# Order of the two projection memory blocks in a fused layernorm, attention and SwiGLU-gate kernel

## Chip, cores and metric

The kernel runs on one core of one Trainium2 chip. The metric is the device time of one execution in microseconds (us), lower is better; the time before is 1717.34 us, the median of three runs from 1717.03 to 1718.39.

## What is computed

Float32 throughout, 2048 tokens of width 512, 32 heads of width 16, a gate of inner width 1792:

```python
xn = layernorm(x)                                 # 2048 x 512
q, k, v = split_heads(xn @ wqkv)                  # 32 heads, 16 wide
s = merge(softmax(q @ k.T * 16**-0.5) @ v) @ wo
g = silu((silu(xn @ w1) * (xn @ w3)) @ w2)        # 512 -> 1792 -> 512
out = x + s * g
```

## The kernel before

Products of float32 values are made from two parts of each value, high and low (suffix `h` and `l`), and three matmuls.

**The projection** (first some 160 us) is the `with` block whose first line the diff touches (L415). It opens two blocks ("pools") of on-chip memory. `pro` holds the eight `wq` tiles (the parts of wqkv, 6 KB per partition each), nine input rows `xin` of 2 KB, some tiny columns and five normalised rows `xn` of 2 KB, 78,240 bytes per partition in all. `pros` holds what leaves the projection: two rows of values `vrow` (2,176 bytes each) and three `sh` and three `sl` of 2 KB, the parts of a block of q or k rows, 16,640 bytes in all. ScalarE copies a finished product from PSUM to `sh` (L575), VectorE makes `sl` (L576), and SyncE's queue stores both to DRAM (L578); for values ScalarE copies to `vrow` (L509), the queue stores that (L510), and ScalarE copies four heads into the resident tile `vt` (L511). The last work of the projection is the value row of the last sixteenth of the tokens: its matmuls (L504), L509, the store L510, L511. Then SyncE's queue loads the next heads' values (`load_v(1)`, L359) and goes on to the gate's weights (L306).

**The main stage** follows without a barrier. When the `with` block ends both its pools are closed, and three pools are opened in their place, one above the other from the same bottom address: `ring` (the later parts of the gate's weights, ten tiles of 2 KB named `wh4`, `wl4` to `wl8`), `work` (24 tiles `pt` for exponentials, and small ones, 59,648 bytes) and `ffn` (the gate's own tiles `th`, `g`, `hs`, `part`). The framework makes the first instruction that uses a new pool wait for the work on every tile of each closed pool that the new one lies over, not only for the tile under its own address.

PE, the tensor engine, takes half-height matmuls in two lanes: `m` (scores for the row maxima, L388, reduced by VectorE in L390), `e` (transposed scores, L624, to which ScalarE applies the exponential into `pt`, L627), `f` (the gate, L855) and, full, `pv` (L637, the exponentials times the values). Their order is a fixed string, `ORDER_OF_ISSUE`; seven PSUM banks are dealt out in that order, and a matmul that begins a bank waits until the engine that reads the bank's last content is done. So PE runs at most seven results ahead of ScalarE and VectorE. GpSimd (POOL) splits raw gate weights `wr` into parts (L320, L321), in order, with the gate's elementwise work (L724, L725, L740 to L742) between. The first four weight units go to tiles that were there before (`xeh`, `xel`); the fifth, `wh4` and `wl4`, is the first in `ring`.

Of the kernel before, what the change touches and what calls it, by code (L numbers as in the profile page):

```python
# [144 lines left out]
def kernel(ctx: ExitStack, tc: tile.TileContext, x, wqkv, wo, w1, w3, w2, out):  # L145
# [266 lines left out]
            nc.sync.dma_start(raw(qs[p % 2])[r:r + 2, c], raw(turned)[16 * h:16 * h + 16, :])  # L412


    with tc.tile_pool(name="pro", bufs=1) as pro, tc.tile_pool(name="pros", bufs=1) as pros:  # L415
        wsp = [[pro.tile([P, 3 * D], F32R, name=f"wq{v}{k}") for v in "hl"] for k in range(KC)]
        xin = [pro.tile([P, D], F32, tag="xin", name=f"xin{t}", bufs=9) for t in range(4)]

# [919 lines left out]
```

## Time and profile before

| | |
|---|---|
| median of three runs | 1717.34 us |
| the profiled execution's own time | 1718.99 us |
| its span, first to last instruction | 1717.2 us |
| mean granted TensorE clock | 0.999 |
| busy: PE, VectorE (DVE), ScalarE (ACT), GpSimd (POOL) | 100%, 84%, 72%, 45% |
| first matmul of the main stage | 159.83 us |

The time is 1.8 us longer than the span. A row of a timeline gives its start, its length, the engine, the line and operation, how many instructions were merged into it, and in brackets how long the engine had been idle and what it waited for. In a table of windows a row is a stretch, its length, then the busy time of PE, PE's weight loads, DVE, ACT and POOL with their instructions, the granted clock, the busy share of the DMA engines and GB/s. A matmul's modelled length overlaps the next: the distance from start to start counts.

### The profile page before, as it was taken

To read this page: it belongs to the slowest core of one execution; us is meant where nothing else is said; L and a number is where in the kernel's file an instruction comes from. 1 tells how busy PE (TensorE), PEld (TensorE's weight loads), DVE (VectorE), ACT (ScalarE), POOL (GpSimd) and SP (SyncE) were. 2 spreads that over 40 slices of the span, in tenths; PEclk is the share of its full clock that TensorE was granted. 3 is DMA by queue.
4 is the path that set the end of the run, shared out by engine and by line. 5 is a ranking of instruction groups with operands and counts; after the bars stand their busy time and mean duration, and the time that the engine had idled before them with its cause. 6 is when DMAs were issued, how large, how long until landed. Compare 5 with 4: busy or idle time off the path is not lost. (4 is left out here: it accounts for less than half of the span.)

```text
span 1717.2 us, 35614 instructions
## 1 busy us (share of the span) xinstructions
PE 1709.9 (100%) x13204; PEld 1095.6 (64%) x13204; DVE 1445.2 (84%) x2477; ACT 1232.4 (72%) x2408; POOL 764.5 (45%) x793
## 2 busy tenths in 40 slices
PE   9999999999999999999999999999999999999999
PEld 8877666666566656566666666566666666665457
DVE  7566999999899889978897898988898989789836
ACT  4223687777878777788777777787778777777971
POOL 3102655255626660566256533664565426542201
PEclk9999999999999999999999999999999999999999
DMA  8756113132323222232332322123512222241722
GB/s 283 250 205 207 58 45 72 33 82 64 77 77 94 70 63 39 60 71 75 88 93 51 73 54 72 45 75 86 118 51 69 64 55 70 68 106 45 248 67 99
DMA packets 146477, 155.36 MB, mean 90 GB/s; under 512 B 41472, under 2 KB 100864, under 8 KB 143328
## 3 DMA queue, kind: packets, MB, share of 16 engines
q1 hardware_dynamic: 145440, 152.04, 31.8%
q8 instruction: 104, 1.70, 0.4%
q10 hardware_dynamic: 864, 1.05, 0.2%
q14 instruction: 69, 0.57, 0.1%
HBM read 107.97 MB, written 44.02 MB: 89 GB/s over the span
## 5 line engine op out<-in xcount | busy, mean ns | idle before, releaser
L390 DVE TENSOR_REDUCE mp<-m 128x1 f32<-128x512 f32 x2048 | 1286.2, 683 | 171.8 <-PE m L388 87.3
L627 ACT ACTIVATE pt<-e 128x512 f32<-128x512 f32 x2048 | 1073.3, 606 | 275.7 <-PE e L624 161.6
L624 PE MATMUL e<-qs,ks 64*128 64x512 f32 x2048 | 719.8, 410 | 0.2
L388 PE MATMUL m<-ks,qs 62*128 62x512 f32 x2048 | 710.5, 416 | 1.8 <-ACT pt L627 1.6
L637 PE MATMUL pv<-pt,vt 128*17 128x512 f32 x4096 | 491.9, 595 | 0.0
L388 PEld LDWEIGHTS m<-ks,qs 62*128 62x128 f32 x2048 | 335.9, 184 | 158.7 <-ACT pt L627 46.3
L624 PEld LDWEIGHTS e<-qs,ks 64*128 64x128 f32 x2048 | 346.5, 185 | 134.2 <-DVE mp L390 35.1
L637 PEld LDWEIGHTS pv<-pt,vt 128*17 128x17 f32 x4096 | 93.2, 96 | 234.5 <-issue 228.7
L855 PE MATMUL f<-xtl,wh 64*128 64x512 f32 x488 | 176.7, 393 | 0.0
L855 PE MATMUL f<-xth,wl 64*128 64x512 f32 x488 | 175.5, 394 | 0.0
L855 PE MATMUL f<-xth,wh 64*128 64x512 f32 x488 | 174.3, 395 | 0.0
L740 POOL TENSOR_TENSOR h<-g,h 128x512 f32<-128x512 f32 x56 | 71.9, 1285 | 201.5 <-ACT h L736 199.7
L855 PE MATMUL f<-wh,hs 64*128 64x512 f32 x496 | 154.8, 393 | 0.0
L855 PE MATMUL f<-xth,xel 64*128 64x512 f32 x408 | 147.7, 398 | 0.0
L855 PE MATMUL f<-xtl,xeh 64*128 64x512 f32 x408 | 147.3, 393 | 0.0
L855 PE MATMUL f<-xth,xeh 64*128 64x512 f32 x408 | 146.6, 395 | 0.0
L855 PE MATMUL f<-xeh,hs 64*128 64x512 f32 x400 | 124.7, 393 | 0.0
L321 POOL TENSOR_TENSOR wl<-wr,wh 128x512 fp32r<-128x512 f32 x92 | 118.5, 1288 | 7.7
L320 POOL TENSOR_SCALAR wh<-wr 128x512 fp32r<-128x512 f32 x92 | 56.9, 618 | 117.6 <-PE f L855 91.6
L321 POOL TENSOR_TENSOR xel<-wr,xeh 128x512 fp32r<-128x512 f32 x76 | 97.9, 1288 | 6.3
L724 POOL TENSOR_SCALAR th<-th 128x512 f32<-128x512 f32 x56 | 34.6, 618 | 127.9 <-ACT th L717 127.8
L855 PE MATMUL f<-wl,hs 64*128 64x512 f32 x248 | 91.4, 392 | 0.0
(175 smaller groups left out, 2065.3 us busy)
## 6 DMA issues: line engine op xcount, KB each, us to landing
wr<-in_B_w_dram SPq DMA_DIRECT2D x168, 256.0 KB
qs<-qk SPq DMA_DIRECT2D x186, 64.0 KB
ks<-qk SPq DMA_DIRECT2D x90, 128.0 KB
qk<-sh SPq DMA_DIRECT2D x32, 256.0 KB
qk<-sl SPq DMA_DIRECT2D x32, 256.0 KB
v<-vrow SPq DMA_DIRECT2D x16, 272.0 KB
xin<-in_A_x_dram SPq DMA_DIRECT2D x16, 256.0 KB
g<-part SPq DMA_DIRECT2D x16, 256.0 KB
```

The costliest lines, as they stand in the source:

```text
L320: nc.gpsimd.tensor_scalar(hi, t, 1.0, 1.0, op0=ALU.mult, op1=ALU.mult)
L321: nc.gpsimd.tensor_sub(lo, t, raw(hi))
L388: nc.tensor.matmul(ps, qs[p % 2][64 * h:64 * h + KM, q0:q0 + P], ks[p % 2][64 * h:64 * h + KM, c * 512:(c + 1) * 512], start=True, stop=True)
L390: nc.vector.reduce_max(mp[p, half][:, h, qt, c:c + 1], ps, axis=AX.X)
L624: nc.tensor.matmul(ps, ks[p % 2][64 * h:64 * h + KR, k * P:(k + 1) * P], qs[p % 2][64 * h:64 * h + KR, q0:q0 + 512], start=True, stop=True)
L627: nc.scalar.activation(pt, ps, AF.Exp, scale=DH ** -0.5)
L637: nc.tensor.matmul(pv[32 * j:32 * j + VW, :], vt[2 * p // GH][:, key, 2 * p % GH + j % 2, :], pt, start=key < 2 if last else k == 0, stop= ...
L724: nc.gpsimd.tensor_scalar(th, th, 1.0, 1.0, op0=ALU.add, op1=ALU.mult)
L740: nc.gpsimd.tensor_mul(h2, g, h2)
L855: nc.tensor.matmul(ps, left[r], right[r], start=starts and lane == 0, stop=ends and lane == 1)
```

## The change

The two pools are opened in the other order; the tiles, the computation and the instructions are the same.

```diff
-    with tc.tile_pool(name="pro", bufs=1) as pro, tc.tile_pool(name="pros", bufs=1) as pros:
+    with tc.tile_pool(name="pros", bufs=1) as pros, tc.tile_pool(name="pro", bufs=1) as pro:
```

What is opened first lies lowest. By the sizes above, counted in bytes per partition from the bottom of the two:

| | before | after |
|---|---|---|
| `pro` | 0 to 78,240 | 16,640 to 94,880 |
| `pros` | 78,240 to 94,880 | 0 to 16,640 |
| `ring` (0 to 20,480) lies over | `pro` | all of `pros`, 3,840 bytes of `pro` |
| `work` (20,480 to 80,128) lies over | `pro`, 1,888 bytes of `pros` | `pro` |
| `ffn` (from 80,128) lies over | `pros` | `pro` |

Every engine's instructions stand in the order they had; what differs is what the first user of each new pool waits for. Of two engines the places are shown, before with a minus and after with a plus. First ScalarE, where the projection ends and the exponentials begin; `DMAHW0` to `DMAHW7` count finished DMAs, the other names in brackets count finished instructions of an engine:

```order
 L509 COPY vrow_250<-m 128x32x16 [waits PE_49]
 L511 COPY vt<-m 128x4x16
-L627 ACTIVATE pt<-e 128x512 [waits DMAHW3_49,DMAHW2_49,DMAHW4_49,DMAHW1_49,DMAHW5_49,DVE_49,DMAHW6_49,PE_49,DMAHW7_49,Activation_49,Pool_49]
+L627 ACTIVATE pt<-e 128x512 [waits PE_49,Pool_49]
 L627 ACTIVATE pt<-e 128x512 [waits PE_49] x15
 L717 ACTIVATE th<-f 128x512 [waits PE_49]
```

The seven DMA counters stood for the last stores of the `sh`, `sl` and `vrow` tiles (L578 and L510), the last value row's among them. The first exponential no longer waits for any of them, only for PE and for GpSimd's last work on the columns of `pro`.

Then GpSimd, at the fifth weight unit:

```order
 L320 TENSOR_SCALAR xeh<-wr 128x512 [waits DMAHW1_49]
 L321 TENSOR_TENSOR xel<-wr,xeh 128x512 [waits Pool_49]
-L320 TENSOR_SCALAR wh_1723<-wr 128x512 [waits DMAHW3_49,DMAHW4_49,DMAHW2_49,DMAHW7_49,DVE_49,PE_49]
+L320 TENSOR_SCALAR wh_1723<-wr 128x512 [waits DMAHW3_49,DMAHW4_49,DMAHW2_49,DMAHW5_49,DMAHW1_49,DMAHW6_49,DMAHW0_49,DMAHW7_49,DVE_49,Activation_49]
 L321 TENSOR_TENSOR wl_1724<-wr,wh_1723 128x512 [waits Pool_49]
 L320 TENSOR_SCALAR wh_1737<-wr 128x512 [waits DMAHW0_49]
```

The split of the fifth unit (`wh_1723` is `wh4`) now waits for those stores; the load of its raw weights (`DMAHW7`) it waited for before and waits for now. Two waits on the same stores go with it: those of GpSimd's first `th` (L724), and of PE's first `pv` (L637). PE's first use of `wl4` (L855) and VectorE's first `rec` (L651) wait for more or fewer of the same stores.

## Prediction

> **What bounds the kernel.** I read the page first, then the waits of PE over the whole span.
>
> ```profile
> span 1717.2 us, 35614 instructions
> PE 1709.9 (100%) x13204; PEld 1095.6 (64%) x13204; DVE 1445.2 (84%) x2477; ACT 1232.4 (72%) x2408; POOL 764.5 (45%) x793
> ...
> PE m L388 <- ACT pt L627: 1.6, 1, 1.6
> PE pv L447 <- POOL minus L442: 1.4, 1, 1.4
> PE m L504 <- ACT wqh L487: 0.2, 1, 0.2
> ```
>
> PE is busy from end to end, and only three of its waits show as idle time. Two belong to the start of the program. The third, 1.6 us behind an exponential, is the only hole that PE has after the first 10 us. Who caused it is asked of line 627 (its releasers), then of ScalarE's timeline and of the DMA queue's.
>
> ```profile
>   DMA v<-vrow: 2.2, 1
> ...
> 160.42 0.22 ACT L511 COPY vt<-m 128x64 f32<-128x64 f32 x1
> 162.88 3.54 ACT L627 ACTIVATE pt<-e 128x512 f32<-128x512 f32 x7 [2.24 <-DMA v<-vrow]
> 167.50 5.12 ACT L627 ACTIVATE pt<-e 128x512 f32<-128x512 f32 x9 [1.08 <-PE f L855]
> ...
> 160.55 0.32 SPq L510 DMA_DIRECT2D v<-vrow  x1
> 162.63 0.37 SPq L359 DMA_DIRECT2D vt<-v  x1
> 163.10 9.28 SPq L306 DMA_DIRECT2D wr<-in_B_w_dram  x6
> ```
>
> Of 2048 exponentials one waited for a store: the first. ScalarE was done with the projection at 160.42 + 0.22 = 160.64 and stood idle 2.24 us until the last value row, issued at 160.55, had landed. This is the wait that the change takes from ScalarE. What it did to PE stands in PE's timeline (one of the two lanes' rows at each start):
>
> ```profile
> 160.17 0.39 PE L624 MATMUL e<-qs,ks 64*128 64x512 f32 x1
> 161.54 0.39 PE L855 MATMUL f<-xth,xeh 64*128 64x512 f32 x1
> 163.53 0.50 PE L388 MATMUL m<-ks,qs 62*128 62x512 f32 x1 [1.59 <-ACT pt L627]
> 163.86 0.39 PE L855 MATMUL f<-xtl,xeh 64*128 64x512 f32 x1
> 164.10 0.39 PE L855 MATMUL f<-xth,xeh 64*128 64x512 f32 x1
> 164.51 0.79 PE L855 MATMUL f<-xth,xel 64*128 64x512 f32 x1
> 165.10 0.63 PE L855 MATMUL f<-xtl,xeh 64*128 64x512 f32 x1
> 165.53 0.63 PE L855 MATMUL f<-xth,xeh 64*128 64x512 f32 x1
> 167.66 0.46 PE L855 MATMUL f<-xtl,xeh 64*128 64x512 f32 x1
> 167.96 0.39 PE L855 MATMUL f<-xtl,xeh 64*128 64x512 f32 x1
> ```
>
> The banks ran out, and nothing began between 161.54 and 163.53. Then the distance from start to start is not 0.23 but 0.43. Windows of one microsecond say why:
>
> ```profile
> 163.00:164.00 1.00, 0.47 (x4) 0.43 (x5) 0.00 (x0) 1.00 (x3) 0.00 (x0) 1.00 0.17 36
> 164.00:165.00 1.00, 1.00 (x8) 0.69 (x6) 0.94 (x2) 1.00 (x3) 0.00 (x0) 0.69 1.16 264
> 165.00:166.00 1.00, 1.00 (x8) 0.70 (x8) 0.35 (x1) 1.00 (x3) 0.00 (x0) 0.50 1.29 272
> 167.00:168.00 1.00, 1.00 (x10) 0.85 (x7) 0.58 (x2) 0.50 (x1) 0.00 (x0) 0.60 1.22 290
> 168.00:169.00 1.00, 1.00 (x11) 0.77 (x9) 1.00 (x2) 0.85 (x3) 0.88 (x2) 1.00 1.22 291
> ```
>
> ```profile
> core 0: 1717.2 us, clock 0.999
> ```
>
> Right behind the hole the granted clock fell to 0.50 for some 3.3 us. That is all that the mean of the span lacks: 0.001 of 1717.2 is 1.7 us, half of 3.3. So the profiled execution paid twice here, and nowhere else.
>
> **The change, part by part.**
>
> *The wait taken from ScalarE.* The first `e` begins at 160.17 and is 0.39 long, so it is there at 160.56, and ScalarE is free at 160.64. I let the first exponential begin at 160.7 instead of 162.88. Seven take 3.54 us, about 0.49 from one to the next, so they end at about 161.3, 161.8, 162.3, 162.8 and on. The `m` that stood at 163.53 needs the bank of the first exponential (it came just behind 162.88 + 0.6); it can go one slot behind the row at 161.54, at 161.77. From there I follow the slots by hand, each 0.23 behind the last unless its bank is late. The next `e` need the second and third exponential's bank and the third maximum's, and find them free: 162.00, 162.23, 162.46, 162.69, 162.92. Then one `m` needs the fifth exponential, whose own `e` was issued at 162.23: it ends at about 163.3, so that slot is 163.35. From here PE goes in step with ScalarE and the maxima: 163.60, 163.85, 164.25, and 164.50 for the slot that was at 167.66. **In the profiled execution that is 3.2 us earlier.**
>
> *How much of it is the hole and how much the clock.* The same count with the first exponential left at 162.88, but at full clock, is paced by the exponentials and reaches that slot at about 166.55. So the slow clock costs 1.1 us and the wait 2.05 us. The 3.3 us at half clock would cost 1.6 us if PE alone set the pace; ScalarE hides a part.
>
> *VectorE* must keep up, since from 168 us it has hardly a gap:
>
> ```profile
> 160.37 1.89 DVE L390 TENSOR_REDUCE mp<-m 128x1 f32<-128x512 f32 x3 [1.79 <-PE m L388]
> 164.06 1.29 DVE L390 TENSOR_REDUCE mp<-m 128x1 f32<-128x512 f32 x2 [1.81 <-PE m L388]
> 166.22 1.29 DVE L390 TENSOR_REDUCE mp<-m 128x1 f32<-128x512 f32 x2 [0.87 <-PE f L855]
> 167.93 6.38 DVE L390 TENSOR_REDUCE mp<-m 128x1 f32<-128x512 f32 x10 [0.42 <-PE f L855]
> ```
>
> Its idle time before 167.93 is 1.81 + 0.87 + 0.42 = 3.1 us. With maxima back to back from 160.37 the eighth starts seven times 0.64 later, at 164.8: 3.1 us earlier. PE's gain can be kept and VectorE's bounds it at 3.1, which I take.
>
> *The wait given to GpSimd.* The fifth weight split now waits for the stores, with two more weight units and the gate's first `th` in order behind it.
>
> ```profile
> 168.03 0.62 POOL L320 TENSOR_SCALAR wh<-wr 128x512 fp32r<-128x512 f32 x1 [17.27 <-PE f L855]
> 168.74 1.29 POOL L321 TENSOR_TENSOR wl<-wr,wh 128x512 fp32r<-128x512 f32 x1
> 173.90 0.62 POOL L724 TENSOR_SCALAR th<-th 128x512 f32<-128x512 f32 x1
> 188.63 0.62 POOL L724 TENSOR_SCALAR th<-th 128x512 f32<-128x512 f32 x1 [3.39 <-ACT th L717]
> ...
> 189.77 0.39 PE L855 MATMUL f<-xth,wl 64*128 64x512 f32 x1
> ```
>
> The view names PE for the 17.27 us, but PE's work on the projection ended by 160; the raw weights were issued at 163.10 behind a load of values, so I take their load to be what ended it at 168.03. The stores had landed by 162.88, since ScalarE waited for all of them. So the added wait is hidden by 5.1 us, and costs nothing. If that cover were gone, `wl4` is written at 170.03 and first read at 189.77, or 186.7 once PE is earlier: 16.7 us more. The waits moved at the first `th`, `pv` and `rec` were past already: nothing either way. The lists of waits change in length too, and what a wait instruction takes stands in the row of those ahead of the exponentials (shortest, median, longest in ns):
>
> ```profile
> L627 ACTq EVENT_SEMAPHORE  x601: 17/17/38, 160.0 to 1668.9; - x151
> ```
>
> ScalarE loses and GpSimd gains a handful, under 0.2 us at the longest either way, once; I take nothing.
>
> *What does not move.* The DMA queue's times at 162.63 and 163.10 follow the last value row and stay, so GpSimd's splits stay at 168.03 to 173.94. The gate's `th` would be ready 3 us earlier and waits for GpSimd there; GpSimd then catches up, because it had 3.39 us idle before 188.63. Nothing that PE needs comes from it sooner.
>
> *The sum.* PE, ScalarE and VectorE wait only for each other from then on, PE has no idle time left to absorb the shift, and loads follow their releases. The profiled execution, 1718.99 us, becomes 1718.99 - 3.1 = 1715.9. The runs without a profile had 1717.03, 1717.34 and 1718.39. Their gap, 1.05 to 1.36 us, has the size of the slow clock's 1.1, so I read the two short ones as executions in which the clock did not fall. For them the wait alone goes: 1717.34 - 2.05 = **1715.3**. The reading is an inference from the sizes; no run shows a clock without a profile.
>
> The row says that a hole of 2.0 us between starts was followed by the half clock. The Trainium skill ("TensorE: Matmul & The Clock Gate", Part 1 and "HAM oscillation") says that the clock is throttled after an idle window of about 3.4 us that runs free of the kernel's start, and that gaps beyond about 3 us are to be avoided. The trace differs on the gap (2.0 us sufficed) and agrees on the length (about 3.3 us slow). By the free-running window the same hole would fall at another place in it each time, which would make the slow clock come and go between runs; by the gap rule the hole would not be its cause, which is the second rival.
>
> **The rivals.**
>
> 1. *Both parts were in every run.* For it: the one trace shows both, and the spread of three runs may be noise. Against it: the spread's size. Then 1717.34 - 3.1 = **1714.2**.
> 2. *The clock falls anyway*, because the change from full to half-height matmuls at 159.83 lowers PE's activity and not the hole. For it: the fall is 4 to 5 us behind that change of work. Against it: half-height pairs run on at 1.00 for the other 1500 us. Then only the wait goes: **1715.3**, or 1716.4 if two of the runs before had been spared the 1.1.
> 3. *The shift is swallowed.* GpSimd and the queue stay where they were, so some weight or q row could be late by what PE gained. Against it: 16.7 us of cover at `wl4`, 3.39 us idle before 188.63. Then about **1717.3**.
> 4. *Slower*: the split of the fifth unit, now behind all stores, holds GpSimd's queue, and with it every later weight part and `hs`. It decides from the point where a store lands more than 16.7 us behind 168.03; each microsecond beyond is a microsecond on PE, and a fall of the clock would add 1.1. It needs a store of over 24 us where the last one took 2.3 (162.88 - 160.55). With one that lands 5.5 us beyond the point the 2.05 us are used up and 3.4 lost: **1720.8**.
>
> That the change does nothing is excluded: the first exponential's wait list is shorter in the built program.
>
> **How the numbers follow.** Forecast, only the wait goes from the median (1715.3): 0.44. Rival 1: 0.34. Rival 2: 0.06. Rival 3: 0.11. Rival 4 and unforeseen losses: 0.05. The range reaches below rival 1 by 0.6 us for VectorE's and the count's roughness and up to 1716.9, which leaves out most of rival 3 and rival 4: 1713.6 to 1716.9. 0.2% is 3.4 us, about what a measurement of this kernel can tell from no change; it is below 1713.9. Rival 1 lies 0.3 us short of it, so I give it half: 0.17 faster, 0.79 within, 0.04 slower.
>
> **What would show it.** In the changed profile the first exponential should begin at about 160.7 with no DMA named; PE should show no idle time at 161.9; the clock should stay 1.00 from 160 to 170; the fifth split should still begin near 168; the slot after ten more should stand 3 us earlier. A fifth split much later than 168, a new idle row on PE before 190, or a clock below 1.00 there would make it wrong; an end that is not earlier although these hold would speak for rival 3.

## The result and the profile after

The changed kernel takes 1714.69 us (median of 22 runs, 1714.22 to 1715.63), the kernel before 1717.20 (22 runs beside them, 1716.66 to 1718.91). The ratio is 0.9984, 95% interval 0.9977 to 0.9990: 2.5 us faster, about 0.15%, and the interval stays below 1. The forecast was 1715.3.

PE's waits over the whole span of the changed kernel, and its releasers and ScalarE's timeline at the place:

```profile
span 1713.0 us, 35608 instructions
...
PE pv L447 <- POOL minus L442: 1.4, 1, 1.4
PE m L477 <- DVE xn L468: 0.2, 1, 0.2
```

```profile
159.53 0.59 ACT L509 COPY vrow<-m 128x512 f32<-128x512 f32 x1 [2.09 <-PE m L504]
160.01 0.22 ACT L511 COPY vt<-m 128x64 f32<-128x64 f32 x1
160.28 8.38 ACT L627 ACTIVATE pt<-e 128x512 f32<-128x512 f32 x16
168.56 0.59 ACT L717 ACTIVATE th<-f 128x512 f32<-128x512 f32 x1
```

The wait of 1.6 us behind an exponential is gone from PE's list, and the store from ScalarE's. The projection ended 0.41 us earlier in this execution (the first matmul of the main stage is at 159.42, not 159.83), so a time of before is to be compared with one of after plus 0.41. On that scale the first exponential begins 2.2 us earlier. Sixteen exponentials now run without a gap, where before they came in groups of seven and nine with a pause of 1.08 us.

The windows of the same place, VectorE's first maxima, and GpSimd's and the DMA queue's rows:

```profile
163.00:164.00 1.00, 1.00 (x10) 0.95 (x11) 1.00 (x3) 1.00 (x3) 0.00 (x0) 1.00 0.69 147
164.00:165.00 1.00, 1.00 (x12) 0.73 (x9) 1.00 (x3) 1.00 (x3) 0.00 (x0) 1.00 1.24 284
165.00:166.00 1.00, 1.00 (x11) 0.81 (x9) 1.00 (x2) 1.00 (x3) 0.00 (x0) 1.00 1.29 258
...
159.96 10.38 DVE L390 TENSOR_REDUCE mp<-m 128x1 f32<-128x512 f32 x17 [1.79 <-PE m L388]
...
162.18 0.37 SPq L359 DMA_DIRECT2D vt<-v  x1
162.65 9.12 SPq L306 DMA_DIRECT2D wr<-in_B_w_dram  x6
...
167.42 0.62 POOL L320 TENSOR_SCALAR wh<-wr 128x512 fp32r<-128x512 f32 x1 [17.49 <-ACT pt L627]
168.12 1.29 POOL L321 TENSOR_TENSOR wl<-wr,wh 128x512 fp32r<-128x512 f32 x1
184.70 0.62 POOL L724 TENSOR_SCALAR th<-th 128x512 f32<-128x512 f32 x1 [2.17 <-ACT th L717]
...
185.84 0.39 PE L855 MATMUL f<-xth,wl 64*128 64x512 f32 x1
```

The granted clock (the column after the five engines) stays at 1.00, and in the windows shown PE, VectorE and ScalarE are busy together. GpSimd's fifth split begins at 167.42, 0.2 us earlier than before once the 0.41 are allowed for, although it now waits for the stores of `sh`, `sl` and `vrow` too. GpSimd's idle time before its second `th` fell from 3.39 to 2.17 us: it has caught up by then, as expected.

### The profile page after: what moved, and what is told of

It is laid out like the page before. It is cut to its first block, busy times and chain, and to the rows that moved or that the text cites. A ratio compares the mean times of both kernels' runs of the same rounds, so it can differ in the third digit from the quotient of the medians.

```text
span 1713.0 us, 35608 instructions
## 1 busy us (share of the span) xinstructions
PE 1707.1 (100%) x13204; PEld 1093.4 (64%) x13204; DVE 1443.9 (84%) x2477; ACT 1232.3 (72%) x2408; POOL 765.9 (45%) x793
## 5 line engine op out<-in xcount | busy, mean ns | idle before, releaser
L637 PE MATMUL pv<-pt,vt 128*17 128x512 f32 x4096 | 491.9, 595 | 0.0
L637 PEld LDWEIGHTS pv<-pt,vt 128*17 128x17 f32 x4096 | 93.2, 96 | 234.8 <-issue 229.3
L855 PE MATMUL f<-xtl,wh 64*128 64x512 f32 x488 | 176.7, 392 | 0.0
L855 PE MATMUL f<-xth,wl 64*128 64x512 f32 x488 | 175.6, 394 | 0.0
L855 PE MATMUL f<-xth,wh 64*128 64x512 f32 x488 | 174.6, 395 | 0.0
L855 PE MATMUL f<-wh,hs 64*128 64x512 f32 x496 | 154.4, 393 | 0.0
L855 PE MATMUL f<-xth,xel 64*128 64x512 f32 x408 | 146.9, 395 | 0.0
L855 PE MATMUL f<-xtl,xeh 64*128 64x512 f32 x408 | 146.8, 392 | 0.0
L855 PE MATMUL f<-xth,xeh 64*128 64x512 f32 x408 | 146.1, 393 | 0.0
L855 PE MATMUL f<-xeh,hs 64*128 64x512 f32 x400 | 124.5, 393 | 0.0
L724 POOL TENSOR_SCALAR th<-th 128x512 f32<-128x512 f32 x56 | 34.8, 621 | 126.5 <-ACT th L717 126.3
L855 PEld LDWEIGHTS f<-xth,wl 64*128 64x128 f32 x488 | 86.4, 185 | 7.6 <-issue 2.6
```

Source lines behind the costliest of these rows:

```text
L637: nc.tensor.matmul(pv[32 * j:32 * j + VW, :], vt[2 * p // GH][:, key, 2 * p % GH + j % 2, :], pt, start=key < 2 if last else k == 0, stop= ...
L724: nc.gpsimd.tensor_scalar(th, th, 1.0, 1.0, op0=ALU.add, op1=ALU.mult)
L855: nc.tensor.matmul(ps, left[r], right[r], start=starts and lane == 0, stop=ends and lane == 1)
```

## Experiments

Two theories were to be told apart. **The wait:** all of the gain is the first exponential's wait for the last store, in two parts, the wait itself and, in a share of the runs, a fall of the clock that the hole in PE's work brings on. **The rivals:** the gain comes from where the tiles lie or from the waits that other engines lost and got; and the clock falls because the work changes at that point, not because PE is idle. The four kernels of the first group ran beside 33 runs of the kernel before (median 1718.11), the three of the second beside 27 (median 1718.15). Every run also lists its mean clock. A mean of 0.999 does not by itself show a fall at the hole: the clock also falls after the last matmul, where it costs nothing (in the changed kernel from 1711.74 on, the last matmul having begun at 1708.90, in a span of 1713.0), and four of the changed kernel's 22 runs have 0.999 at 1714.40 to 1714.57. In both sets of the kernel before, though, every run with 0.999 took longer than every run with 1.000, so there the two parts of the runs can be told apart by the clock.

### The wait taken away without the exchange

```diff
-        xin = [pro.tile([P, D], F32, tag="xin", name=f"xin{t}", bufs=9) for t in range(4)]
+        xin = [pro.tile([P, D], F32, tag="xin", name=f"xin{t}", bufs=9) for t in range(4)]; pro.tile([P, 512], F32, name="pad")
```

> The order of before, with one unused 2 KB tile more in the projection's other block. It lifts the block of row parts and value rows by 2 KB, so the 1,888 bytes of it that the exponentials' pool lay over are under it no longer, and nothing else moves: the later weight parts stay over the projection's weights. Theory of the wait: the first exponential's wait for the stores is all that the change took away, so this alone gives the time of after, 1714.7 us, no hole on PE at 162 and a clock of 1.00. Rival (the gain comes from where the tiles lie, or from the waits that GpSimd, PE and VectorE lost or got): the weight parts and the blocks lie as before, GpSimd waits as before, so it stays at 1717.2 us.

Measured: 1714.67 us (11 runs, 1713.99 to 1714.91), ratio to before 0.9981, interval 0.9972 to 0.9990. ScalarE's timeline and PE's waits of this kernel:

```profile
PE pv L447 <- POOL minus L442: 1.4, 1, 1.4
PE m L504 <- ACT wqh L487: 0.2, 1, 0.2
...
159.86 0.22 ACT L511 COPY vt<-m 128x64 f32<-128x64 f32 x1
160.14 8.37 ACT L627 ACTIVATE pt<-e 128x512 f32<-128x512 f32 x16
```

The whole gain, with the blocks in the order of before and GpSimd's wait as before. So neither the place of the weight parts nor GpSimd's wait is needed for it; the 1,888 bytes by which the exponentials' pool reached over the block of rows were the whole matter. By the sizes the first `pv` and `rec`, which use the same pool, lose their waits for the stores here too; the first `pv` before the change began at 172.4, long after the stores had landed by 162.88, so its wait was past.

### The wait given back to the exchanged order

```diff
-        xin = [pro.tile([P, D], F32, tag="xin", name=f"xin{t}", bufs=9) for t in range(4)]
+        xin = [pro.tile([P, D], F32, tag="xin", name=f"xin{t}", bufs=9) for t in range(4)]; pros.tile([P, 1024], F32, name="pad")
```

> The order of after, with one unused 4 KB tile more in the block of row parts, so that it reaches under the exponentials' pool and the first exponential waits for the stores again, while the weight parts lie over that block as in after. Theory of the wait: back to the time of before, 1717.2 us as a median, with single runs near 1717.05 and near 1718.5 us, and a hole of some 1.8 us on PE at 162. Rival (placement, or the other engines' waits): it stays at 1714.7 us.

Measured: 1717.18 us (1716.71 to 1718.87), ratio to before 0.9997, interval 0.9988 to 1.0006. Seven of the eleven runs have a clock of 1.000 and 1716.94 us in the mean, four have 0.999 and 1718.59. By the sizes the block now reaches 256 bytes under the exponentials' pool (16,640 + 4,096 - 20,480). PE's first wait, ScalarE's row and a window:

```profile
PE m L388 <- ACT pt L627: 1.5, 1, 1.5
...
162.76 3.54 ACT L627 ACTIVATE pt<-e 128x512 f32<-128x512 f32 x7 [2.19 <-DMA v<-vrow]
...
165.00:166.00 1.00, 1.00 (x8) 0.81 (x6) 0.23 (x1) 1.00 (x3) 0.00 (x0) 0.50 1.28 272
```

The exchange gains nothing when the wait is there. The hole and the half clock came back with it.

### The wait doubled, before and after

The last value row is stored twice; the second store waits for the first. The edit is the same in both kernels:

```diff
-            nc.sync.dma_start(v_d[t], vrow[t % 2].rearrange("p h d -> p (h d)"))
+            for _ in range(1 + (t == NT - 1)): nc.sync.dma_start(v_d[t], vrow[t % 2].rearrange("p h d -> p (h d)"))
```

In the kernel before:

> The kernel before, with the last value row stored twice, the second store behind the first: the suspected wait is doubled. Theory of the wait: the first exponential begins some 2.3 us later, the hole on PE is near 4 us, and with so long a hole the clock falls in every run: 1717.05 + 2.3 + 1.5 = 1720.8 us. If the fall of the clock has nothing to do with the hole, it comes in the same share of runs as before: 1719.4 as a median with some runs at 1720.9. Rival (the store is not what counts): 1717.2 us.

Measured: 1721.26 us (1720.08 to 1722.35), ratio to before 1.0018, interval 1.0009 to 1.0027. The mean clock is 0.998 in six runs (1721.79 us in the mean) and 0.999 in five (1720.56). PE's wait, ScalarE's row, and two windows of the profiled execution, which is one of the six:

```profile
PE m L388 <- ACT pt L627: 3.6, 1, 3.6
...
164.42 2.06 ACT L627 ACTIVATE pt<-e 128x512 f32<-128x512 f32 x4 [4.24 <-DMA v<-vrow]
...
164.00:165.00 1.00, 0.00 (x0) 0.00 (x0) 0.00 (x0) 0.58 (x2) 0.00 (x0) 0.66 0.00 0
170.00:171.00 1.00, 1.00 (x8) 0.83 (x6) 0.47 (x1) 0.60 (x1) 0.92 (x2) 0.50 1.22 289
```

The hole grew from 1.6 to 3.6 us, and no run has a clock of 1.000. Here the slow stretch began inside the hole and lasted to 171, about 6.8 us, twice as long as before. With the wait alone 2.0 us longer (4.24 against 2.24) and no fall of the clock, 1717.06 + 2.0 = 1719.1 would stand; every run lies about 1.0 us or more over that. The five runs at 0.999 lie 1.5 over it in the mean and the six at 0.998 2.7, which fits one and two slow stretches, though only one trace shows it. The expected 1720.8 had one stretch in every run and came out 0.5 us too low.

In the changed kernel:

> The changed kernel with the last value row stored twice. Theory of the wait: only GpSimd's fifth weight split and the loads behind the stores come some 2.3 us later, and they have over 15 us of cover: 1714.7 us, unchanged. Rival (GpSimd's new wait or the queue behind the stores bounds the time after the change): 1716 to 1717 us.

Measured: 1714.86 us (1714.24 to 1715.38), ratio to before 0.9983, interval 0.9974 to 0.9992. GpSimd's fifth split and the loads in this kernel:

```profile
164.88 1.34 SPq L306 DMA_DIRECT2D wr<-in_B_w_dram  x1
...
169.79 0.62 POOL L320 TENSOR_SCALAR wh<-wr 128x512 fp32r<-128x512 f32 x1 [19.39 <-DMA wr<-in_B_w_dram]
```

The loads and the split came 2.2 to 2.4 us later than after the change (162.65, 167.42), and the median rose by 0.2 us, within the scatter of the runs. The changed kernel does not feel the store. The rows also settle what the split waits for: it begins 4.9 us behind the issue of its weights here (169.79 - 164.88), 4.8 after the change (167.42 - 162.65) and 4.9 before it (168.03 - 163.10). It is the load, which this view now names, and not PE or ScalarE, as the views of before and after have it.

### The hole filled with work

The wait stays; PE is given 62-row matmuls (seven, then three) just ahead of the hole, into a bank that is overwritten later.

```diff
-    late = []
+    late = []; fill = lambda: [nc.tensor.matmul(pv, qs[0][64:64 + KM, 0:P], ks[0][64:64 + KM, 0:512], start=True, stop=True) for _ in range(7)]
...
-    for c in ORDER_OF_ISSUE:
-        settle()
+    for n, c in enumerate(ORDER_OF_ISSUE):
+        settle(); n == 13 and fill()
```

With seven:

> The kernel before with seven matmuls more, which PE issues just ahead of the hole into a bank that is not in use yet and whose result is overwritten: the wait of the first exponential stays, the hole on PE is filled with 7 x 0.23 = 1.6 us of work. Theory (an idle PE is what makes the clock fall): the clock is 1.00 in every run and all runs lie in the lower group of before, 1717.05 us. Rival (the clock falls because the work changes from full to half-height matmuls, whether PE waits or not): clocks of 0.999 in about half of the runs, the groups of 1717.0 and 1718.5 us stay as in before.

Measured: 1717.10 us (1716.55 to 1717.83), ratio to before 0.9995, interval 0.9986 to 1.0004. Ten runs have 1.000. The eleventh, 0.999 at 1717.10, is the profiled one. Its clock is 1.00 behind the hole and falls only at 1713.5, 2 us after its last matmul, which costs nothing. PE's wait, ScalarE's row, two windows at the place and two at the end:

```profile
PE m L388 <- ACT pt L627: 0.5, 1, 0.5
...
162.72 8.33 ACT L627 ACTIVATE pt<-e 128x512 f32<-128x512 f32 x16 [2.23 <-DMA v<-vrow]
...
164.00:165.00 1.00, 1.00 (x10) 0.65 (x8) 1.00 (x2) 1.00 (x3) 0.00 (x0) 1.00 1.20 271
165.00:166.00 1.00, 1.00 (x11) 0.74 (x9) 0.81 (x3) 1.00 (x3) 0.00 (x0) 1.00 1.29 273
...
1713.00:1714.00 1.00, 0.00 (x0) 0.00 (x0) 0.00 (x0) 0.00 (x0) 0.00 (x0) 0.77 0.57 194
1714.00:1715.00 1.00, 0.00 (x0) 0.00 (x0) 0.00 (x0) 0.00 (x0) 0.00 (x0) 0.50 0.04 11
```

The change of work is there, the wait is there, only the idle time is cut to 0.5 us, and the upper group of before (13 of 27 runs at 1718.71 in the mean) is gone. So the idle time brings the clock down, not the change of work. What is left is the price of the wait at full clock.

With three:

> As the kernel with seven filling matmuls, with three: 0.7 us of the hole are filled and 1.1 us stay. Theory of idle time within a window that runs free of the program: the shorter the hole, the smaller the share of runs in which the clock falls, so clearly fewer than the 21 of 33 of before, perhaps none; the other runs at 1717.05 us. Rival (any hole at the change of work will do): the same share as before, near 1717.0 and 1718.5 us.

Measured: 1717.03 us (1716.40 to 1718.26), ratio to before 0.9996, interval 0.9987 to 1.0004. Two of eleven runs have 0.999 and 1718.1 and 1718.3 us. The three ran beside the other lane's matmuls, so the hole shrank by less than was meant: PE's wait in the profiled run, one of the nine at full clock, was 1.4 us.

```profile
162.91 0.49 PE L388 MATMUL m<-ks,qs 62*128 62x512 f32 x1 [1.44 <-ACT pt L627]
```

The share fell, from 34 of 60 runs of before in the two groups to 2 of 11; with eleven runs that is a direction and no measure.

### The last store taken out of the block

```diff
-        vrow = [pros.tile([P, H, VW], F32, name=f"vrow{i}") for i in range(2)]
+        vrow = [pros.tile([P, H, VW], F32, name=f"vrow{i}") for i in range(2)] + [room_v(1)[:, 0:8].rearrange("p t h d -> p (t h) d")]; slot = lambda t: 2 if t == NT - 1 else t % 2
...
-            nc.scalar.copy(vrow[t % 2][:, :, 0:DH], v)
-            nc.sync.dma_start(v_d[t], vrow[t % 2].rearrange("p h d -> p (h d)"))
+            nc.scalar.copy(vrow[slot(t)][:, :, 0:DH], v)
+            nc.sync.dma_start(v_d[t], vrow[slot(t)].rearrange("p h d -> p (h d)"))
...
-        nc.sync.dma_start(room_v(g), v_d[:, :, g * GH * VW:(g + 1) * GH * VW].rearrange("t p (h d) -> p t h d", h=GH))
+        nc.sync.dma_start(vt[g] if g in vt else room_v(g), v_d[:, :, g * GH * VW:(g + 1) * GH * VW].rearrange("t p (h d) -> p t h d", h=GH))
```

> The kernel before, but the last of the sixteen value rows goes through a tile outside the projection's blocks (the room of the next heads' values, free at that time), so that the first exponential still waits for the stores of both blocks, the latest of which is now that of the last sl part, issued 1.95 us earlier. Theory: of seven stores that were waited for only the last one to land counts; the first exponential begins near 161.0, some 0.3 us late, PE has banks enough to run through it, no hole, clock 1.00: 1714.7 to 1715.0 us. Rival (waiting for seven DMA counters costs time by itself, or all of the stores land together): 1716 us or more with a hole.

Measured: 1715.35 us (1714.78 to 1716.25), ratio to before 0.9986, interval 0.9977 to 0.9995. All eleven runs have 1.000.

```profile
160.82 8.33 ACT L627 ACTIVATE pt<-e 128x512 f32<-128x512 f32 x16 [0.40 <-PE e L624]
```

ScalarE waits 0.40 us for the first exponential, PE has no hole, and yet the time is 0.7 us over that of the changed kernel (0.35 over the upper end that I expected). So the last store alone made the hole; but the spare banks do not make a short delay free. Since ScalarE runs sixteen exponentials without a gap from there, the start of the first is the start of all: counted from the first matmul of the main stage (159.61 here, 159.42 after the change), the first exponential comes 0.35 us later than after the change and ScalarE's first `th` (L717), at 169.05, 0.30 later. What ended the 0.40 us is not shown. The view names an `e` that was done by 160.34; the store of the last `sl`, issued at 158.38, is the likely one.

## Why the prediction was right

- **Which wait, and that it goes:** right. The first exponential began at 160.28, which is 160.69 on the clock of before; 160.7 was forecast. No DMA is named, PE has no hole.
- **The wait given to GpSimd costs nothing:** right, shown from two sides. Without it the time is the same (the 2 KB pad), and with the store 2.3 us later still (the doubled store after).
- **What the wait costs at full clock, 2.05 us:** a little undersized. At the place itself the filled kernel, which has the wait at full clock, reaches ScalarE's first `th` (L717) at 170.95, the changed kernel at 168.56; counted from the first matmul of the main stage (159.68 and 159.42) that is 2.1 us. In the times it is 2.2 to 2.5: the seven filling matmuls against the changed kernel give 1717.09 - 1714.67 = 2.4 in the mean, and in the first group the runs of before at full clock (1717.06) lie 2.5 over the padded kernel and 2.2 over the one with the doubled store. Times of different sets agree no better than to 0.3 us, since the kernel before at full clock has 1717.06 in the first group and 1717.35 in the second, which ran on another chip. My count let PE set slots of 0.23 us and both lanes step together. In fact the lanes part, and in the filled kernel ScalarE runs sixteen exponentials without a gap while VectorE has idle time, so ScalarE's delay of 2.2 us counts almost in full.
- **What the fall of the clock costs, 1.1 us:** undersized. Runs of before at 0.999 lie 1.4 us over those at 1.000 in both groups (1718.44 and 1717.06; 1718.71 and 1717.35), 1.6 when the wait was given back. In the profiled execution the two came to 3.5 us (the first `th`, 172.51 before, 168.56 + 0.41 after), not 3.2; less the 2.1 of the wait, that leaves the same 1.4. VectorE's bound of 3.1 did not hold: I took 0.64 us for a maximum, and seventeen without a gap took 10.38, that is 0.61.
- **That the clock falls in some runs only, and that the median had not paid for it:** right, and now shown rather than inferred, since each run of the experiments lists its clock; rival 1, both parts in every run, falls with it. The time alone would not have told them apart: 1714.69 lies 0.5 us over rival 1's 1714.2 and 0.6 under the forecast, whose wait was sized too small. Among the 22 runs beside the result six lie from 1718.07 up and sixteen at 1717.34 or less. In the later groups it was 34 of 60, so there the median of before lay above 1718, and the padded kernel of the first group gains 3.4 us against it: the size of this gain depends on a share that differs from one set of runs to another, and what sets it was not found. That the median on record, and that of the 22 runs, came from the lower part was luck: with a share like that of the later groups the gain would have been near 3.4 us and nearer to rival 1's 3.1 than to the forecast's 2.05.
- **Rival 2, the clock falls anyway:** excluded by the filled hole, and by the changed kernel itself, whose work changes at the same place and whose clock stays at 1.00 there. **Rival 3, the shift is swallowed:** excluded, the end moved by at least as much as the place itself. **Rival 4:** its condition never came near; `wl4` was written at 169.41 and first read at 185.84.

A hole of 3.6 us lowered the clock in 11 of 11 runs, one of 1.5 to 1.6 in 38 of 71 (the kernel before in both groups, and the wait given back), one of 1.4 in 2 of 11, one of 0.5 in none of 11; the lengths are those of the profiled executions. In the traces' records of the clock the slow stretch lasts 3.413 us in the kernel before and with the wait given back, and 6.827 us with the doubled store. The times between the changes of the clock within a trace, up to the fall after the last matmul, are whole multiples of 3.413 us in all nine traces (157.013 us is 46 of them, 1706.664 is 500), whether there is a hole or not. So the clock changes on a grid of 3.413 us whose start shifts from run to run. On this grid the hole before (161.94 to 163.53) lies whole between two marks (160.96 and 164.38), and so does the one with the wait given back. The hole of the run with three matmuls, 161.47 to 162.91 at full clock, is cut by a mark at 161.96. That fits a clock which falls only when enough idle time lies between two marks; with so few traces the least idle time that is enough is not found, nor why the slow stretch of the doubled store lasted two of the steps.

The Trainium skill ("TensorE: Matmul & The Clock Gate", Part 1) has a window of about 3.4 us that runs free of the program and throttles after an idle one. The traces agree on its length and on the free run. They differ on how much of it must be idle, and from the advice ("HAM oscillation") against gaps above some 3.4 us: 1.5 to 1.6 us between two marks was enough here.

## What to carry to other kernels

When a stage ends and its pools are closed, look at which of the new pools lies over a block whose last work is a store: the first instruction of the new pool waits for the landing, 2.2 us here. An overlap of 1,888 bytes was enough, and by the sizes 256 bytes where the wait was given back. Let such a block lie under a pool whose first use is late. A short hole in a dense matmul stream can cost about twice its length (1.6 us of hole and 3.5 us in all in the profiled execution here), because the clock may fall behind it. Where runs of one kernel fall into two groups, compare their mean clocks before averaging them, and look in the trace where the clock fell: a fall after the last matmul lowers the mean too and costs nothing.

## Not expected

- A hole of 1.5 us on PE was enough to halve the clock for a whole stretch of 3.4 us, in about half of the runs.
- A delay of the first exponential of 0.40 us without any hole on PE still cost time: 0.30 us at ScalarE's first `th`. The medians differ by 0.7 us; they come from different sets of runs, and such sets differ by 0.3 us with the same kernel, so the rest is not shown to come from the delay.
